# Layer norms on GpSimd a group ahead, earlier first FFN weights and a regrouped filler list in a fused attention and SwiGLU forward and backward

## The chip, the cores and the metric

One core of one Trainium2 chip. The metric is the device time of one execution in microseconds (us). Each kernel was timed in several executions on the same chip as the kernel before. A clock lies beside every execution: the mean clock that was granted to TensorE, as a share of full speed (0.96 to 0.97 in all runs of this study). The runs were made in batches, each on another chip; kernels of different batches are compared through their ratios to the kernel before.

Names used below: PE is TensorE, DVE is VectorE, ACT is ScalarE, POOL is GpSimd, SP is SyncE, which only issues DMAs here, in order. An eviction is the instruction, mostly on DVE, that copies a finished matmul result (`gen`) into another tile.

## The reference, cut to what matters

The kernel returns the output of a block and the gradients of its six inputs that it uses. Sizes: S = 2048 rows, D = 448, 16 heads of 28, F = 1792; bf16.

```python
def _fwd_reference(A_x, A_wqkv, A_wo, B_x, B_w_gate, B_w_up, B_w_down):
    xn = layernorm(A_x)                       # no scale, no bias
    q, k, v = split(xn @ A_wqkv)              # 16 heads of 28
    o = softmax(q @ k.T * 28 ** -0.5) @ v
    ffn = (silu(xn @ B_w_gate) * (xn @ B_w_up)) @ B_w_down
    return A_x + o @ A_wo + ffn               # B_x is not used

out, vjp = jax.vjp(_fwd_reference, ...)
return out, *vjp(grad_out)                    # gradients of A_x, A_wqkv, A_wo, B_w_gate, B_w_up, B_w_down
```

## The kernel before: what the change and the argument touch

The kernel has a forward part of 256 *slots* and a backward part. A slot is one tile of 128 keys against 512 queries of a group of four heads: four score matmuls on PE, then the exponentials on ACT. In the time that ACT needs for a slot, PE does other work, the *fillers*: projections of later head groups, the FFN (units a, u, dh, dw), transposes. Fillers wait in one list, `items`. They give a nominal cost in ns when they yield, and each slot spends a budget of it:

```python
    def pump(self, budget, slot):
        self.debt = min(self.debt + budget, 2 * budget)
        while self.debt > 0 and self.step(slot):
            pass
    ...
    FWD_NS = 1780
    ...
    def slot(i):
        ...                                   # 4 score matmuls, 3 exponentials
        fill.pump(FWD_NS, i)
```

So list and budget fix the order of all instructions when the program is built. At run time every engine goes through its own queue in that order and waits where data or a buffer is missing.

The filler list, first part (cut):

```python
    items = []
    for t in range(NT):                       # NT = 16
        items.append(lambda t=t: T_unit(dyT, dy_t, t))       # dy transposes
    chain = [(fc, sc) for fc in range(NFC) for sc in range(4)]
    LEAD = 2

    def ug(b, j):
        if j == 1:
            gate_ops(*chain[0])
        if j < len(chain):
            gate_ops(*chain[j])
        yield from u_unit(*b)
    for i in range(len(chain) + LEAD):
        if i < len(chain):
            items.append(lambda a=chain[i]: a_unit(*a))      # gate projection, tanh
        k = i - LEAD
        if k >= 0:
            b = chain[k]
            items.append(lambda b=b, j=i - 1: ug(b, j))      # up projection
            items.append(lambda b=b: dh_unit(*b))            # dy @ w_down.T
            if b[0] > 0 and b[1] < 3:
                items.append(lambda b=b: dw_unit(b[0] - 1, b[1]))   # weight gradients
    ...
    for g in range(G - 1, 0, -1):             # projections of groups 1..3, inserted from place lo on
        lo, hi = max(int(n_it * (g - 0.85) / 4), 26), int(n_it * (g - 0.1) / 4)
```

A weight-gradient unit reads a transposed activation `f_sp` that SP's queue has brought, and evicts through a tile with a single buffer:

```python
    def dh_unit(fc, sc):
        ...
        sp_transpose(fsp[fc][:, sc]..., t3[:]...)            # f_sp <- hda, through SP
        SP.dma_start(out=F_d[sc, :, fc], in_=t3[:])          # store of hda
    def dw_unit(fc, w):
        ...                                                  # 16 matmuls on f_sp
        if w == 0:
            o = wk.tile([P, D], BF16, name="dw_o", bufs=1)
            DVE.tensor_copy(out=o[:], in_=ps[:, :D])
            SP.dma_start(out=out_6[fc * P:(fc + 1) * P, :], in_=o[:])
```

The layer norm and the opening, twelve slots in which the rows arrive in four groups of four tiles:

```python
    def ln_norm(t):
        DVE.tensor_scalar(out=xn_sp[:, t, :], in0=xn_sp[:, t, :],
                          scalar1=mv[:, t, 0:1], scalar2=rstd[:, t:t + 1],
                          op0=ALU.subtract, op1=ALU.mult)
    ...
    slot(0)
    proj(2, 0)
    norm4(1)              # four ln_norm
    T(4, 5)               # transposes
    slot(1)
    T(6, 7)
    proj(1, 1)
    stats4(2)             # four ln_stats, then rstd on GpSimd
    slot(2)
    proj(2, 1)
    slot(3)
    ...                   # groups 2 and 3 likewise; before slot 7:
    for g in range(G):
        SP.dma_start_transpose(out=woT[:, :, g * P:(g + 1) * P], in_=wo_pad[:, g, :])
    load_fw(0)            # first FFN weights
    ...
    slot(11)
    fill.stream = [(0, u) for u in items[:10]]
    proj(0, 1)
    slot(12)
    store_wqT(0)
    proj(0, 2)
    slot(13)
    proj(0, 3)
    slot(14)
    fill.stream += [(0, u) for u in items[10:]]
    slot(15)
```

The softmax here doesn't subtract the row's maximum and nothing guards it: scores larger than these inputs give would overflow.

## Time and profile before

| | kernel before |
|---|---|
| median of the first three runs | 1489.7 us (1489.18 to 1491.23) |
| the execution that was profiled | 1484.67 us, span 1482.9, clock 0.969 |
| start of slot 12 (profile) | 49.9 us |
| start of slot 29 | 100.7 us |
| first row of the backward part | 628.2 us |

Slot 12 ends the opening, and slot 29 lies where PE has become the limit. Slot starts are read from the first score matmul of the slot in the timeline; the first backward row is the first `sb` matmul. The table of stretches, cut at these three times, shows for each engine its busy time and, in brackets, its instructions; then the clock granted to PE, the share of DMA engines busy and GB/s:

```profile
core 0: us, PE busy (x) PEld busy (x) DVE busy (x) ACT busy (x) POOL busy (x), PEclk, DMA share, GB/s
0.00:49.90 49.90, 31.39 (x184) 11.93 (x185) 30.29 (x81) 25.78 (x39) 17.49 (x43) 0.83 0.53 125
49.90:100.70 50.80, 41.75 (x322) 17.31 (x322) 35.29 (x67) 37.12 (x60) 26.37 (x44) 0.93 0.91 202
100.70:628.20 527.50, 498.13 (x3580) 192.11 (x3579) 327.92 (x569) 471.76 (x732) 217.16 (x286) 0.99 0.71 170
628.20:1482.90 854.70, 781.23 (x8593) 325.05 (x8592) 751.29 (x1304) 728.66 (x1352) 85.55 (x109) 0.97 1.00 191
```

PE is busy for 498 of 527.5 us in the third stretch: that part is bound by PE. It is busy for 73 of the first 100.7 us, partly at a lower clock: the opening is not. The end of a matmul in such a trace is worked out, not observed (the Trainium skill, Perfetto Trace Analysis, Tensor Engine Instruction, says the same); so PE's busy time is used here for comparisons only.

One group of the opening in the timeline. A line starts with its start, then its duration (both us); at the end, in brackets, the idle time of the engine before it and what released it:

```profile
27.48 0.23 POOL L226 TENSOR_SCALAR rstd<-mv 128x4 f32<-128x4 f32 x1 [12.02 <-DVE mv L231]
27.79 1.04 POOL L227 TENSOR_TENSOR rstd<-rstd,m_half 128x4 f32<-128x4 f32 x1
...
29.96 1.31 DVE L234 TENSOR_SCALAR xn_t<-xn_t,mv,rstd 128x448 bf16<-128x448 bf16 x4
30.40 0.84 PE L312 MATMUL gen<-ident_bf,xn_t 128*128 128x128 bf16 x8 [1.13 <-DVE xn_t L234]
```

Four norms take DVE 1.31 us together, and PE waits 1.13 us for them. The largest hole of PE follows later:

```profile
62.54 1.48 POOL L212 MEMSET wq_g<- 128x384 bf16 x4 [15.94 <-DMA wqT_st<-wq_g]
...
70.54 0.61 POOL L364 TENSOR_SCALAR nn<-tt 128x512 f32<-128x512 f32 x1
...
73.87 0.63 ACT L355 ACTIVATE tt<-ag 128x512 f32<-128x512 f32 x1 [5.50 <-POOL nn L366]
...
75.46 0.61 PE L583 MATMUL s_w<-QQ,KK 32*128 32x512 bf16 x2 [5.93 <-ACT eT L586]
```

GpSimd sat 15.94 us before a clear of weights; the first gate operation (`nn<-tt`, L364) came behind it in its queue at 70.54; ACT's tanh waited for a tile that the gate frees; PE waited 5.93 us for ACT. The groups by form put numbers to single operations (busy us, then mean ns of one, then idle before):

```profile
L364 POOL TENSOR_SCALAR nn<-tt 128x512 f32<-128x512 f32 x56 | 34.8, 621 | 42.4 <-DVE hda L393 17.5 <-ACT eT L588 17.4 <-ACT eT L586 4.7
L234 DVE TENSOR_SCALAR xn_t<-xn_t,mv,rstd 128x448 bf16<-128x448 bf16 x16 | 5.6, 410 | 0.8 <-POOL rstd L227 0.8
```

A norm takes DVE 410 ns. There is no norm on GpSimd here; the nearest thing is the 128x512 `nn<-tt`, 621 ns. Last, the turn from forward to backward, where the fillers are used up (SPq is SP's queue of DMAs):

```profile
609.92 1.88 PE L404 MATMUL gen<-xn_t,f_sp 128*128 128x448 bf16 x9
...
617.47 0.53 SPq L690 DMA_DIRECT2D kd<-KD_d  x1
...
628.19 0.61 PE L780 MATMUL sb<-kd,qd 32*128 32x512 bf16 x2
```

The last filler runs at 609.92, the backward part's first load is issued at 617.47, and its first row starts at 628.19.

### The profile page before, as it was taken

The numbers are of one execution on the slowest core, as the hardware profiler recorded it, in microseconds if no ns is written. First come the engines' busy times: TensorE is split into PE (matmuls) and PEld (weight loads), VectorE is DVE, ScalarE is ACT, GpSimd is POOL, SyncE is SP. The second block draws the span as 40 slices with busy tenths as digits, with TensorE's granted clock in tenths as the row PEclk, the third lists the DMA queues.
The fourth block names the chain that finished last, engine by engine and source line by source line (L and its number), as shares of the span: only waits on it lengthen the run. The fifth ranks groups of instructions, "written<-read, shape, count | busy, mean of one in ns | idle before, by whom it ended". The sixth has DMA issues, their size and how long they took to land. (4 is left out here: it accounts for less than half of the span.)

```text
span 1482.9 us, 34360 instructions
## 1 busy us (share of the span) xinstructions
PE 1352.5 (91%) x12672; PEld 546.4 (37%) x12672; DVE 1144.8 (77%) x2020; ACT 1263.3 (85%) x2180; POOL 346.6 (23%) x481
## 2 busy tenths in 40 slices
PE   5799999999999999889998889999999998999984
PEld 2333333333333333333433334433343343443341
DVE  6577666666666666388988878888989998999977
ACT  4689989988998889788988878999889998989953
POOL 2555533363434353000101001001011010000113
PEclk8999999999999999898999999999999999999997
DMA  4887956786688665599999999999999999999951
GB/s 126 173 201 192 208 129 167 184 200 146 170 189 189 150 147 141 148 197 203 208 207 199 210 200 191 203 210 225 211 177 204 196 211 209 195 199 212 178 114 51
DMA packets 698591, 269.55 MB, mean 182 GB/s; under 512 B 618080, under 2 KB 674104, under 8 KB 698424
## 3 DMA queue, kind: packets, MB, share of 16 engines
q1 hardware_dynamic: 693448, 261.24, 85.6%
q0 software_dynamic: 3568, 5.83, 1.8%
q8 instruction: 99, 1.62, 0.5%
q14 instruction: 68, 0.56, 0.1%
q10 hardware_dynamic: 1408, 0.30, 0.1%
HBM read 63.99 MB, written 58.85 MB: 83 GB/s over the span
## 5 line engine op out<-in xcount | busy, mean ns | idle before, releaser
L815 DVE TENSOR_TENSOR ds_sb<-db,e_sb 128x512 bf16<-128x512 f32 x1024 | 647.6, 684 | 65.7 <-PE db L788 23.5
L807 ACT ACTIVATE e_sb<-sb 128x512 bf16<-128x512 f32 x1024 | 554.1, 611 | 57.3 <-PE db L788 42.9
L586 ACT ACTIVATE eT<-s_w 128x1024 bf16<-128x1024 f32 x256 | 263.2, 1028 | 54.6 <-PE s_ps L583 51.2
L588 ACT ACTIVATE eT<-s_ps 128x512 bf16<-128x512 f32 x512 | 280.0, 611 | 0.0
L788 PE MATMUL db<-kd,qd 32*128 32x512 bf16 x1024 | 242.6, 386 | 12.8 <-DVE ds_sb L815 11.3
L780 PE MATMUL sb<-kd,qd 32*128 32x512 bf16 x1024 | 213.9, 390 | 6.9 <-DMA kd<-KD_d 2.9
L912 POOL TENSOR_TENSOR dq_acc<-dq_acc,dq_st 128x256 f32<-128x256 f32 x64 | 46.4, 725 | 579.8 <-ACT dq_st L910 579.8
L870 PE MATMUL acc<-ds_sb,qd 128*32 128x512 bf16 x1024 | 163.0, 395 | 0.0
L866 PE MATMUL acc<-e_sb,qd 128*32 128x512 bf16 x1024 | 161.0, 395 | 0.4 <-DVE dw_o L510 0.4
L853 ACT COPY dsT<-db 128x1024 bf16<-128x1024 bf16 x128 | 130.2, 1017 | 24.7 <-PE db L852 24.0
L583 PE MATMUL s_ps<-QQ,KK 32*128 32x512 bf16 x512 | 124.7, 390 | 4.1
L365 POOL TENSOR_TENSOR nn<-nn,ag 128x512 f32<-128x512 f32 x56 | 71.1, 1269 | 233.2 <-DVE ag L363 232.2
L1079 PE MATMUL genb<-wguT,dau_c 128*128 128x448 bf16 x448 | 117.9, 357 | 5.9 <-ACT dq_st L910 3.8
L583 PE MATMUL s_w<-QQ,KK 32*128 32x512 bf16 x512 | 101.3, 391 | 21.6 <-ACT eT L586 18.8
L780 PEld LDWEIGHTS <-qd 32*128 32x128 bf16 x1024 | 48.6, 91 | 150.9 <-issue 140.1
L404 PE MATMUL gen<-xn_t,f_sp 128*128 128x448 bf16 x448 | 99.1, 354 | 1.0 <-DVE hda L393 0.6
L404 PEld LDWEIGHTS <-f_sp 128*128 128x128 bf16 x672 | 59.8, 98 | 75.3 <-issue 25.9
L897 PE MATMUL genb<-dsT,kd 128*32 128x256 bf16 x2048 | 81.5, 280 | 6.3 <-DVE y L1031 2.8
L852 PE MATMUL db<-ident_bf,ds_sb 128*128 128x128 bf16 x1024 | 80.2, 222 | 1.8 <-DVE ds_sb L815 1.8
L852 PEld LDWEIGHTS <-ds_sb 128*128 128x128 bf16 x1024 | 68.9, 100 | 27.1 <-issue 8.4
L583 PEld LDWEIGHTS <-KK 32*128 32x128 bf16 x1024 | 29.1, 91 | 126.7 <-issue 125.6
L441 DVE TENSOR_TENSOR oacc<-gen,oacc 128x512 f32<-128x512 f32 x48 | 33.2, 691 | 53.2 <-PE gen L433 53.1
(155 smaller groups left out, 1929.0 us busy)
## 6 DMA issues: line engine op xcount, KB each, us to landing
F_d<-hda SPq DMA_DIRECT2D x56, 384.0 KB, 3.1
dau_c<-F_d SPq DMA_DIRECT2D x56, 256.0 KB, 3.7
h_c<-F_d SPq DMA_DIRECT2D x24, 256.0 KB, 3.3
qd<-QD_d SPq DMA_DIRECT2D x24, 256.0 KB, 3.8
dc<-dqkvT_d SPq DMA_DIRECT2D x12, 384.0 KB, 5.0
dsT<-ds_sb SPq DMA_TRANSPOSE x256, 4.8
wT_d<-wT_f SPq DMA_DIRECT2D x14, 256.0 KB
KD_d<-qk_sp SPq DMA_DIRECT2D x7, 512.0 KB, 3.5
```

Of the source, the lines that this page charges most:

```text
L404: PE.matmul(ps[:, :D], lhsT=fsp[fc][:, t // 4, w, t % 4, :], rhs=rhs[:, t, :], start=(t == 0), stop=(t == NT - 1))
L583: PE.matmul(sp4[hh], lhsT=KK[g][r:r + HP, kt * P:(kt + 1) * P], rhs=QQ[g][r:r + HP, qsl], start=True, stop=True, tile_position=(r, 0))
L586: ACTE.activation(out=e2[0][:], in_=wide[:], func=ACT.Exp, scale=SCALE)
L588: ACTE.activation(out=e2[1][:, j], in_=sp4[2 + j], func=ACT.Exp, scale=SCALE)
L780: PE.matmul(s_ps[:], lhsT=qside[g, qc][r:r + HP, 0, qi * P:(qi + 1) * P], rhs=kside[g, kc][r:r + HP, 0, :], start=True, stop=True, tile_po ...
L788: PE.matmul(d_ps[:], lhsT=qside[g, qc][r:r + HP, 1, qi * P:(qi + 1) * P], rhs=kside[g, kc][r:r + HP, 1, :], start=True, stop=True, tile_po ...
L807: ACTE.activation(out=est[k][:, j], in_=sps.pop((k, j))[:], func=ACT.Exp, scale=SCALE)
L815: DVE.tensor_tensor(out=ds[:, qi % 2, j], in0=dps.pop((k - 1, j))[:], in1=est[k - 1][:, j], op=ALU.mult)
L852: PE.transpose(ps[:, c, :], ds[:, 1, c // 4, (c % 4) * P:(c % 4 + 1) * P], ident_bf[:])
L853: ACTE.copy(out=dsT[b][:, 3].rearrange("p j kt s -> p (j kt) s"), in_=ps[:])
L866: PE.matmul(a[r:r + HP, :], lhsT=sp4[:, 1, r:r + HP], rhs=e[:, j, :], start=first, stop=last, tile_position=(0, r), skip_group_check=True)
L870: PE.matmul(a[r:r + HP, :], lhsT=sp4[:, 0, r:r + HP], rhs=ds[:, qi % 2, j, :], start=first, stop=last, tile_position=(0, r), skip_group_ch ...
```

## The change

Its intent: shorten the opening. The norms of groups 1 to 3 leave DVE for GpSimd and are issued a group ahead; the first FFN weights are asked for before anything else of the FFN; the weights' transposes (`woT`) are spread over the groups so that V's come ahead of them; two Q projections and twelve of the 16 dy transposes become ordinary fillers behind the first FFN units, so that the FFN chain starts two slots earlier; the first gate is issued early so that GpSimd does not block it. In addition the budget of a slot is lowered, to make the fillers last through the last slot, group 1's projections start later in the list (`LO`), and weight-gradient units of the last FFN block are moved. The core of the diff, with cuts marked:

```diff
+LO = 44
-    def ln_norm(t):
-        DVE.tensor_scalar(out=xn_sp[:, t, :], in0=xn_sp[:, t, :],
+    def ln_norm(t, eng=DVE):
+        eng.tensor_scalar(out=xn_sp[:, t, :], in0=xn_sp[:, t, :],
                           scalar1=mv[:, t, 0:1], scalar2=rstd[:, t:t + 1],
                           op0=ALU.subtract, op1=ALU.mult)
  # ... K's transposed store deferred by a list `later`; load_fw(0) split into load and fw_T(0)
         if w == 2:
             o = dwo2.pop(fc)
+            sp_flush()
     items = []
-    for t in range(NT):
+    for t in range(4):
         items.append(lambda t=t: T_unit(dyT, dy_t, t))
+    for sc in range(2, 4):
+        items.append(lambda sc=sc: qkv_unit(0, 0, sc))
     def ug(b, j):
-        if j == 1:
-            gate_ops(*chain[0])
  # ... in the loop over the chain:
+        if i == 1:
+            items.append(lambda: gate_ops(*chain[0]) or iter(()))
+            if k < 3:
+                for t in range(4 * k + 4, 4 * k + 8):
+                    items.append(lambda t=t: T_unit(dyT, dy_t, t))
-            if b[0] > 0 and b[1] < 3:
-                items.append(lambda b=b: dw_unit(b[0] - 1, b[1]))
+            if b[0] == NFC - 1:
+                todo = {1: (0,), 3: (1, 2)}.get(b[1], ())
+            else:
+                todo = (b[1],) if b[0] > 0 and b[1] < 3 else ()
+            for w in todo:
+                items.append(lambda b=b, w=w: dw_unit(b[0] - 1, w))
-        lo, hi = max(int(n_it * (g - 0.85) / 4), 26), int(n_it * (g - 0.1) / 4)
+        lo, hi = max(int(n_it * (g - 0.85) / 4), LO), int(n_it * (g - 0.1) / 4)
-    FWD_NS = 1780
+    FWD_NS = 1720
     def norm4(cc):
+        ln_rstd(cc)
         for t in range(4 * cc, 4 * cc + 4):
-            ln_norm(t)
+            ln_norm(t, POOL)
+    load_fw(0)
+    norm4(1)
     proj(1, 0, True)
     proj(0, 0)
+    for c in range(3):
+        k = 4 * c
+        t = 4 * c + 4
+        slot(k)
+        if c == 0:
+            proj(2, 0)
+        if c < 2:
+            ln_stats(t + 4)
+            ln_stats(t + 5)
+        slot(k + 1)
+        T(t, t + 1)
+        if c < 2:
+            ln_stats(t + 6)
+        slot(k + 2)
+        T(t + 2, t + 3)
+        proj(1, c + 1)
+        if c < 2:
+            ln_stats(t + 7)
+            norm4(c + 2)
+        slot(k + 3)
+        proj(2, c + 1)
+        if c == 0:
+            fw_T(0)
+        for u in later:
+            u()
+        woT_load(c)
+    store_wqT(0)
     proj(0, 1)
+    fill.stream = [(0, u) for u in items]
+    for k in range(12, 16):
+        slot(k)
+        if k == 13:
+            woT_load(3)
  # ... the old sequence of slots 0 to 15 is removed
```

More of the change, by code (lines that the diff above doesn't have):

```diff
@@ L298, in qkv_unit @@
                 st = wk.tile([P, S], BF16, name="qk_sp", bufs=1)
-                sp_transpose(st[:].rearrange("p (t r) -> p t r", r=P), src[:], nat,
+                put = lambda: sp_transpose(st[:].rearrange("p (t r) -> p t r", r=P), src[:], nat,
                              (dst[:, :, 2, :].rearrange("c p s -> p c s"),
                               st[:].rearrange("p (c s) -> p c s", c=4)))
+                if g == 0 and tq == 1:
+                    later.append(put)
+                else:
+                    put()
             elif g > 0:
@@ L338, in load_fw, with fw_T @@
         POOL.dma_start(out=w[:, 2, :D], in_=B_w_down[fsl, :])
-        sp_transpose(wT[:].rearrange("p a c d -> p (a c) d"), w[:].rearrange("p a n -> p (a n)"),
-                     (wT_d[:, fc], wT[:, 0:2].rearrange("p a c d -> p a (c d)")))
-        fw[fc] = (w4[:, 0], w4[:, 1], wT[:, 2])
+        fw[fc] = (w4[:, 0], w4[:, 1], wT[:, 2], lambda: sp_transpose(
+            wT[:].rearrange("p a c d -> p (a c) d"), w[:].rearrange("p a n -> p (a n)"),
+            (wT_d[:, fc], wT[:, 0:2].rearrange("p a c d -> p a (c d)"))))
+        if fc > 0:
+            fw_T(fc)
+    def fw_T(fc):
+        fw[fc][3]()
+    later = []
     def a_unit(fc, sc):
@@ L537 @@
             items.append(lambda b=b: dh_unit(*b))
-            if b[0] > 0 and b[1] < 3:
-                items.append(lambda b=b: dw_unit(b[0] - 1, b[1]))
+            if k < 3:
[3 more added lines that the diff above has]
+                todo = {1: (0,), 3: (1, 2)}.get(b[1], ())
+            else:
+                todo = (b[1],) if b[0] > 0 and b[1] < 3 else ()
+            for w in todo:
+                items.append(lambda b=b, w=w: dw_unit(b[0] - 1, w))
     for w in range(3):
@@ L612, in stats4, with norm4 @@
             ln_stats(t)
+        norm4(cc)
+    def norm4(cc):
         ln_rstd(cc)
-    def norm4(cc):
         for t in range(4 * cc, 4 * cc + 4):
-            ln_norm(t)
+            ln_norm(t, POOL)
     ln_stats(4)
-    norm4(0)
+    for t in range(4):
+        ln_norm(t)
     for t in range(4):
@@ L627, with woT_load @@
         ln_stats(t)
-    ln_rstd(1)
+    load_fw(0)
+    norm4(1)
     proj(1, 0, True)
     proj(0, 0)
-    slot(0)
-    proj(2, 0)
-    norm4(1)
-    T(4, 5)
-    slot(1)
-    T(6, 7)
-    proj(1, 1)
-    stats4(2)
-    slot(2)
-    proj(2, 1)
-    slot(3)
-    slot(4)
-    norm4(2)
-    T(8, 9)
-    slot(5)
-    T(10, 11)
-    proj(1, 2)
-    stats4(3)
-    slot(6)
-    proj(2, 2)
-    for g in range(G):
-        SP.dma_start_transpose(out=woT[:, :, g * P:(g + 1) * P], in_=wo_pad[:, g, :])
-    load_fw(0)
-    slot(7)
-    slot(8)
-    norm4(3)
-    T(12, 13)
-    slot(9)
-    T(14, 15)
-    proj(1, 3)
-    slot(10)
-    proj(2, 3)
-    slot(11)
-    fill.stream = [(0, u) for u in items[:10]]
-    proj(0, 1)
-    slot(12)
-    store_wqT(0)
-    proj(0, 2)
-    slot(13)
-    proj(0, 3)
-    slot(14)
-    fill.stream += [(0, u) for u in items[10:]]
-    slot(15)
+    def woT_load(g):
+        SP.dma_start_transpose(out=woT[:, :, g * P:(g + 1) * P], in_=wo_pad[:, g, :])
+    for c in range(3):
[25 more added lines that the diff above has]
+    store_wqT(0)
+    proj(0, 1)
+    fill.stream = [(0, u) for u in items]
[3 more added lines that the diff above has]
+            woT_load(3)
     qside, kside = {}, {}
```

## The prediction

> **What bounds the kernel now.** One core, 1489.7 us. The table of stretches shows four regimes. From 101 to 612 us (attention forward, FFN work as fillers between slots) PE is busy 486.3 of 510.5 us at clock 1.00: PE-bound, 2.31 us a slot; ACT needs only about 1.87 us a slot (seen where the fillers had run out). The opening is not: from 16.2 to 101.2 us PE is busy 68 of 85 us, part of it at granted clocks of 0.75 and 0.90. From 612 to 628 us the fillers are used up and PE is busy 11.3 of 16.5 us at clock 0.64. The backward and tail after that (855 us) are not touched.
>
> **What the opening loses (timeline, waits).** Twelve slots take 33.7 us. Each group of four waits for statistics, rstd (GpSimd pow, 1.04 us), four norms on DVE (1.3 us), transposes, evictions, projections. The largest hole is 69.5 to 75.5 us: the waits name ACT, but GpSimd had sat 15.9 us (46.6 to 62.5) before clearing the next projection weights, waiting for the wq transpose; the first gate operation started only at 70.5, so tanh and the filler banks stood still.
>
> **What the change does.**
> - Norms of groups 1 to 3 go to GpSimd, a group ahead. No norm there is in this trace; a one-input 128x512 operation took 0.62 us, a two-input one 1.27. Estimate: 0.6 us each, 3.8 us a group with rstd, against about 10 us available. The Trainium skill (GPSIMD Engine Reference, 4.1) calls one-input operations roughly line-rate; this agrees. PE's wait for norms (3.4 us in three) goes. I expect slot 12 at 46 instead of 49.9 us: the chain transposes, evictions, projection remains.
> - Twelve of 16 dy transpose tiles and two Q projections move behind the first FFN units; the FFN chain starts in slot 13 instead of 15, its first gate is issued before the next weights, the next group's projection weights come at filler 28 instead of 10. The 15.9 us wait and the 6 us hole should vanish. At 2.3 us a slot, slot 29 starts at 85.5 instead of 101.2 us: -15.7 us. But by the instruction order 3 us less filler work is then done.
> - Filler budget 1780 to 1720 ns a slot; total PE work is the same. By the instruction order the fillers now last through slot 255, with 45 weight-gradient matmuls (8.5 us at 0.19) after it; before, the last six slots had none. That uses some 6 us of lost PE time. But the backward's first loads wait for the last filler: before, 10.6 us passed from there to the first qd's landing; about 5 us of that becomes bare PE idleness.
>
> Sum: last filler at 85.5 + 510.5 + 3.1 + 3.0 (score and output matmuls of six slots) = 602 us; backward's first row at 612.7 instead of 628.2: -15 us, less 1.5 us for collisions.
>
> **Predicted: 1476 us, 1468 to 1485 (8 in 10).** Faster by over 2%: 0.03; within 2%: 0.96; slower: 0.01.
>
> **What would show it.** Slot 29 near 85 us; no PE hole over 2 us between 50 and 80 us; clock above 0.85 from 20 to 50 us; no 16 us GpSimd wait; GpSimd norm near 0.6 us; first backward row near 613 us; backward 855 us.
>
> **What would make it wrong.** GpSimd norms slow or blocked by DVE (over 1.5 us); PE staying cold in the opening (the Trainium skill, TensorE: Matmul & The Clock Gate, Part 1: an idle window of about 3.4 us throttles it); twelve projections now bunched in slots 38 to 50 stalling; a longer bubble at the turn.

## The result, and the profile after

| | before | after | predicted |
|---|---|---|---|
| median | 1489.4 us (1487.16 to 1491.23, 4 runs) | 1504.3 us (1502.22 to 1506.15, 4 runs) | 1476 (1468 to 1485) |
| slot 12 | 49.9 | 58.0 | 46 |
| slot 29 | 100.7 | 102.5 | 85.5 |
| first backward row | 628.2 | 643.4 | 612.7 |
| from there to the end | 854.7 | 861.0 | 855 |

The ratio is 1.010, with a 95% interval of 1.0078 to 1.0123: slower, though within 2%. A ratio is here always the mean time of a kernel's runs over the mean of the runs of the kernel before in the same rounds, so it is not quite the ratio of the medians quoted. The executions that were profiled lie 21.5 us apart and not 15: that of before (1484.67) is a further execution, faster than all four of the table, and that of after is the slowest of its four (1506.15). The traces split the 21.5 us into 8.1 before slot 12, 7.1 from there to the first backward row, and 6.2 after it; how far such a split can be trusted is said under the table of the experiments.

The table of stretches of the kernel after, cut at its own slots 12 and 29 and its first backward row (columns as above):

```profile
0.00:58.00 58.00, 32.86 (x181) 12.27 (x184) 27.34 (x69) 26.85 (x40) 36.84 (x51) 0.74 0.40 104
58.00:102.50 44.50, 37.48 (x302) 15.63 (x307) 33.61 (x63) 35.95 (x57) 27.08 (x38) 0.96 0.97 213
102.50:643.40 540.90, 496.75 (x3537) 191.68 (x3589) 332.59 (x573) 470.99 (x732) 222.12 (x296) 0.99 0.71 164
643.40:1504.40 861.00, 784.67 (x8594) 326.19 (x8592) 751.51 (x1305) 728.97 (x1352) 85.56 (x109) 0.96 1.01 192
```

GpSimd's work to slot 12 has doubled, 17.5 to 36.8 us, and PE's clock there has fallen from 0.83 to 0.74. In the third stretch PE needs about the same busy time as before (496.75 against 498.13) for a stretch 13.4 us longer. A caution: in this stretch the trace lacks some 50 matmuls (3537, where there are 3589 weight loads); busy time and idle time of PE are therefore not compared to within a few us between the two, but elapsed time is.

One group of the opening in the timeline:

```profile
27.33 0.75 DVE L290 TENSOR_SCALAR KK<-gen,cols 128x512 bf16<-128x512 f32 x1 [1.96 <-PE gen L273]
28.00 0.62 DVE L231 BATCH_NORM_STATS2 stats<-xn_t 128x6 f32<-128x448 bf16 x1
...
28.92 0.23 POOL L227 TENSOR_SCALAR rstd<-mv 128x4 f32<-128x4 f32 x1 [4.78 <-DVE mv L232]
29.24 1.04 POOL L228 TENSOR_TENSOR rstd<-rstd,m_half 128x4 f32<-128x4 f32 x1
...
30.38 7.39 POOL L235 TENSOR_SCALAR xn_t<-xn_t,mv,rstd 128x448 bf16<-128x448 bf16 x4
...
34.15 0.61 PE L317 MATMUL gen<-ident_bf,xn_t 128*128 128x128 bf16 x4 [1.50 <-POOL xn_t L235]
```

Two things are to be seen. Four norms take GpSimd 7.39 us, not 2.4; the transposes wait for each of them. Up to slot 12 PE waits 11.0 us in ten places for GpSimd's norms, where before it waited 3.4 us in three for DVE's. And they do not run a group ahead: GpSimd was idle for 4.78 us, because the last statistics of the group stand in DVE's queue behind the eviction of K (`KK<-gen`, 27.33), which itself waits for the previous group's projection. So a group takes 13.6 us: 1.46 from the start of rstd to the first norm, 7.39 for the norms, 4.78 idle. The groups by form:

```profile
L376 POOL TENSOR_SCALAR nn<-tt 128x512 f32<-128x512 f32 x56 | 35.2, 628 | 61.6 <-DVE hda L405 41.1 <-ACT tt L367 15.5 <-ACT eT L610 2.9
L235 POOL TENSOR_SCALAR xn_t<-xn_t,mv,rstd 128x448 bf16<-128x448 bf16 x12 | 22.2, 1858 | 0.3
```

The operation that the estimate was taken from kept its time (628 ns); the norm takes 1858 ns, three times that, on fewer elements and bf16. The hole near 70 us is gone, as intended: the largest idle time of PE between 50 and 80 us is 1.85 us. The turn:

```profile
631.11 0.39 PE L605 MATMUL s_w<-QQ,KK 32*128 32x512 bf16 x2
...
633.91 6.22 PE L416 MATMUL gen<-xn_t,f_sp 128*128 128x448 bf16 x32
...
637.41 0.53 SPq L709 DMA_DIRECT2D kd<-KD_d  x1
...
643.43 0.39 PE L799 MATMUL sb<-kd,qd 32*128 32x512 bf16 x2
```

The fillers now last through the last slot, and the first load of the backward part (637.41) is issued while they still run. From the last filler's end (640.1) to the first backward row 3.3 us pass. The turn got shorter, but everything before it is late.

### The profile page after: what moved, and what is told of

It is laid out like the page before. It is cut to its first block, busy times and chain, and to the rows that moved or that the text cites. A ratio compares the mean times of both kernels' runs of the same rounds, so it can differ in the third digit from the quotient of the medians.

```text
span 1504.4 us, 34282 instructions
## 1 busy us (share of the span) xinstructions
PE 1351.8 (90%) x12611; PEld 545.8 (36%) x12672; DVE 1145.0 (76%) x2008; ACT 1262.8 (84%) x2180; POOL 371.6 (25%) x493
## 3 DMA queue, kind: packets, MB, share of 16 engines
q1 hardware_dynamic: 693448, 261.24, 85.5%
## 5 line engine op out<-in xcount | busy, mean ns | idle before, releaser
L605 PE MATMUL s_w<-QQ,KK 32*128 32x512 bf16 x512 | 102.2, 395 | 16.6 <-ACT eT L608 13.6
L799 PEld LDWEIGHTS <-qd 32*128 32x128 bf16 x1024 | 48.6, 91 | 150.1 <-issue 139.2
L416 PEld LDWEIGHTS <-f_sp 128*128 128x128 bf16 x672 | 59.9, 98 | 79.7 <-issue 30.8
L446 PE MATMUL gen<-eT,VS 128*32 128x512 bf16 x1024 | 69.4, 393 | 4.3 <-DVE hda L405 1.6
```

Source lines behind the costliest of these rows:

```text
L416: PE.matmul(ps[:, :D], lhsT=fsp[fc][:, t // 4, w, t % 4, :], rhs=rhs[:, t, :], start=(t == 0), stop=(t == NT - 1))
L605: PE.matmul(sp4[hh], lhsT=KK[g][r:r + HP, kt * P:(kt + 1) * P], rhs=QQ[g][r:r + HP, qsl], start=True, stop=True, tile_position=(r, 0))
L799: PE.matmul(s_ps[:], lhsT=qside[g, qc][r:r + HP, 0, qi * P:(qi + 1) * P], rhs=kside[g, kc][r:r + HP, 0, :], start=True, stop=True, tile_po ...
```

## The experiments

Seventeen kernels were run; all gave correct results. Names with a_ start from the kernel after, names with b_ from the kernel before. In the expectations, letters stand for the theories and rivals named there. One thing in them was put too strongly: some compare "39 against 23 us" of PE idle time in the forward part. The traces of after, a_dve, a_early, a_muladd, a_dve_lo26, a_1780, b_1720, b_forms and b_forms2 hold 58 to 62 matmuls fewer than the other traces (12672), and what is missing then looks like idle time. What follows from the runs is therefore read from elapsed time for the same work and from times, or from single waits.

All measured numbers in one table, for reference below. "12 to row" is the elapsed time from slot 12 to the first backward row.

| kernel | median us | ratio to before (95%) | slot 12 | slot 29 | first row | 12 to row |
|---|---|---|---|---|---|---|
| before | 1489.4 | | 49.9 | 100.7 | 628.2 | 578.3 |
| after | 1504.3 | 1.0100 (1.0078 to 1.0123) | 58.0 | 102.5 | 643.4 | 585.4 |
| a_dve | 1495.0 | 1.0043 (1.0004 to 1.0081) | 48.8 | 94.4 | 633.8 | 585.0 |
| a_early | 1494.9 | 1.0046 (1.0013 to 1.0080) | 50.1 | 95.8 | 638.2 | 588.1 |
| a_muladd | 1494.5 | 1.0064 (1.0033 to 1.0094) | 46.0 | 92.0 | 632.1 | 586.1 |
| a_1780 | 1504.2 | 1.0119 (1.0079 to 1.0159) | 57.9 | 108.0 | 644.0 | 586.1 |
| a_dve_1780 | 1490.9 | 1.0030 (1.0005 to 1.0055) | 49.2 | 100.1 | 637.2 | 588.0 |
| a_dve_lo26 | 1496.4 | 1.0072 (1.0045 to 1.0099) | 48.6 | 98.0 | 639.3 | 590.7 |
| a_muladd_1780 | 1492.2 | 1.0044 (1.0000 to 1.0088) | 44.1 | 93.1 | 632.3 | 588.2 |
| b_1720 | 1510.2 | 1.0154 (1.0128 to 1.0181) | 50.9 | 103.6 | 651.9 | 601.0 |
| b_gate | 1489.6 | 1.0022 (0.9992 to 1.0052) | 48.9 | 106.2 | 632.9 | 584.0 |
| b_norm | 1479.3 | 0.9947 (0.9921 to 0.9973) | 46.0 | 95.1 | 627.4 | 581.4 |
| b_open | 1488.4 | 1.0005 (0.9978 to 1.0032) | 44.1 | 98.7 | 632.5 | 588.4 |
| b_norm_1720 | 1501.6 | 1.0094 (1.0051 to 1.0138) | 44.2 | 96.2 | 640.5 | 596.3 |
| b_norm_1720_o2 | 1490.8 | 1.0037 (1.0006 to 1.0067) | 45.8 | 98.0 | 632.5 | 586.7 |
| b_norm_q | 1487.7 | 1.0015 (0.9965 to 1.0064) | 45.0 | 92.0 | 628.5 | 583.5 |
| b_norm_dw | 1492.9 | 1.0044 (1.0002 to 1.0085) | 44.2 | 97.9 | 635.2 | 591.0 |

The slot columns are one execution each. Slot 29 has not the same filler work behind it where budget or order differ (3 us less is ordered by then at 1720), so that column is compared with care.

How far one trace differs from the next can be read from b_forms and b_forms2 (below), which have the forward part of the kernel before unchanged: slot 12 at 50.2 and 50.6, slot 29 at 101.4 in both, the first row at 632.1 and 631.7, and 581.9 and 581.1 us from slot 12 to it. So the trace of before is a fast one, and differences of up to some 4 us in the last two columns are not shown by one trace each: the 7.1 us of the change between slot 12 and the first row are 3.5 to 4.3 us against these two, and b_norm's first row is 4.3 to 4.7 us earlier, not 0.8. Likewise slot 12 lies between 44.1 and 46.0 in the eight kernels that have the opening of a_muladd.

### First: is the opening's loss the norm's engine, its place, or the budget?

**a_dve**: the norms back on DVE, all else as in the change.

```diff
-            ln_norm(t, POOL)
+            ln_norm(t)
```

> The changed kernel with the norms of groups 1 to 3 back on DVE, all else as changed. Theory A (the GpSimd norm, 1.86 us where 0.6 was estimated, sits on the opening's chain): slot 12 starts at 46 to 49 us instead of 58.0, the time falls from 1504 to 1491-1496 us. Rival B (the new order of stats, transposes and projections is what holds the opening, whatever engine norms): slot 12 stays at 55 us or later and the time within 4 us of 1504. The part of the loss that comes after slot 29 should stay in both.

Measured: slot 12 at 48.8, 9.2 us before the change's, and 1495.0 us. The norm's engine costs about 8.5 us by the ratios (1.0100 less 1.0043, of some 1489). With it undone the kernel is still slower than before: elapsed time from slot 12 to the first row is 585.0, as in the change (585.4).

**a_early**: the slow norms stay on GpSimd, but their statistics come ahead of the transposes, and they are issued before the K projection.

```diff
-            ln_stats(t + 4)
-            ln_stats(t + 5)
+            for u in range(t + 4, t + 8):
+                ln_stats(u)
         slot(k + 1)
         T(t, t + 1)
-        if c < 2:
-            ln_stats(t + 6)
         slot(k + 2)
         T(t + 2, t + 3)
-        proj(1, c + 1)
         if c < 2:
-            ln_stats(t + 7)
             norm4(c + 2)
+        proj(1, c + 1)
```

> The changed kernel, norms still on GpSimd, but the four stats of a group before the transposes of the one before, and its rstd and norms put in right after those transposes, ahead of the K projection. Theory A1 (GpSimd stood idle 4.8 us a group because its inputs, the last stats, are queued behind the K eviction, so the norms are not a group ahead in fact): the period of a group falls from 13.6 to 9-10 us, slot 12 at 46 to 49 us, time 1491-1497 us, though each norm still takes 1.86 us. Theory A2 (1.86 us a norm is too slow in any order): slot 12 at 54 us or later, time 1500 us or more.

Measured: slot 12 at 50.1 and 1494.9 us, nearly what a_dve gave. The two groups that follow one another so took 8.8 and 11.4 us instead of 13.6. So two things were needed for the loss together: an operation of 1.86 us, and statistics that reach it late. Either one mended recovers most of it.

**a_1780**: the change with the old budget.

```diff
-    FWD_NS = 1720
+    FWD_NS = 1780
```

> The changed kernel with the filler budget back at 1780 ns. Theory C (the lower budget costs the steady forward: after it PE idles 39 us instead of 23 us between slots 29 and 255): idle there falls to 20-28 us, the fillers end some 6 slots before the last, the time falls by 5 to 12 us to 1492-1499. Rival D (the extra idle has nothing to do with the budget but with where units fall): idle stays above 33 us and the time within 4 us of 1504.

Measured: 1504.2 us, no different from the change. On the kernel after, the budget is worth nothing in the time. That is not so for other kernels below. Its trace shows two more things. Slot 12 comes at 57.9 with the same opening at a clock of 0.82, so the clock of 0.74 in the trace of after cost no time there. And slots 12 to 29 take 50.1 us, where the change took 44.5 and the kernel before 50.8: the shortening of this stretch comes with the lower budget (a_dve and a_dve_1780 show the same, 45.6 and 50.9).

### Second: why is the norm slow on GpSimd?

**b_forms**: the kernel before with 18 GpSimd operations appended at its end, where DVE and PE are idle; it measures the cost of forms by itself.

```diff
+    sm = dict(op0=ALU.subtract, op1=ALU.mult)
+    ... POOL.tensor_scalar(out=xb, in0=xb, scalar1=pa, scalar2=pb, **sm)       # x3: bf16, per-row operands
+    ... POOL.tensor_scalar(out=xb, in0=xb, scalar1=0.5, scalar2=0.5, **sm)     # x3: bf16, constants
+    ... POOL.tensor_scalar(out=xo, in0=xf, scalar1=pa, scalar2=pb, **sm)       # x3: f32, per-row
+    ... POOL.tensor_scalar(out=xo, in0=xf, scalar1=0.5, scalar2=0.5, **sm)     # x3: f32, constants
+    ... POOL.tensor_scalar(out=xb, in0=xb, scalar1=pa, scalar2=None, op0=ALU.mult)  # x3
+    ... POOL.tensor_scalar(out=xb[:, :224], ..., scalar1=pa, scalar2=pb, **sm) # x3: half the width
```

> The kernel before with 18 extra GpSimd operations of one input at its very end, six forms three times each, with DVE idle (its total time does not matter, some 20 us more). 128x448: bf16 in and out with two per-partition pointer scalars; the same with constants; f32 with pointers; f32 with constants; bf16 with one pointer and one operation; bf16 128x224 with two pointers. If contention with DVE made the norm slow in the opening, the first form takes 0.6-0.9 us here; if the form itself is slow, 1.8 us again. If pointers are the cost, constants take 0.6 us in both types; if bf16 is, f32 takes 0.6 us with pointers as well.

Measured (one run, 1517.4 us, the 18 operations being appended), groups by form; L1308 is the norm's own form, L1314 f32 with constants, L1316 the single multiply, L1318 half the width:

```profile
L1308 POOL TENSOR_SCALAR e_sb<-e_sb,rstd 128x448 bf16<-128x448 bf16 x3 | 5.6, 1865 | 0.2
...
L1314 POOL TENSOR_SCALAR e_sb<-e_sb 128x448 f32<-128x448 f32 x3 | 5.1, 1708 | 0.3
L1316 POOL TENSOR_SCALAR e_sb<-e_sb,rstd 128x448 bf16<-128x448 bf16 x3 | 4.2, 1403 | 0.2
L1318 POOL TENSOR_SCALAR e_sb<-e_sb,rstd 128x224 bf16<-128x224 bf16 x3 | 3.3, 1112 | 0.3
```

Neither the element type (1859 in f32 with per-row operands) nor the per-row operands (1710 against 1865) nor contention with DVE, which is idle there, makes it slow. From 224 to 448 columns it grows by 753 ns: 3.36 ns per column (a column is one element in each of the 128 rows). What is left is the pair of operations: the 621 ns operation of before is a multiply and an add.

**b_forms2**: the same with other pairs.

```diff
+    ... op0=ALU.mult, op1=ALU.add         # x3, per-row;   then x3 with constants
+    ... op0=ALU.mult, op1=ALU.subtract    # x3, per-row
+    ... op0=ALU.add, op1=ALU.mult         # x3, per-row
+    ... op0=ALU.add                       # x3, one operation, per-row
+    ... op0=ALU.mult                      # x3, one operation, constant
```

> The kernel before with 18 more one-input GpSimd operations at its end, DVE idle. The first set took 1.7 to 1.9 us in every type whether with pointers or constants, yet the gate's multiply-then-add of 128x512 f32 with constants takes 0.62 us. Theory E (the pair of operations decides: subtract-then-multiply is on a slow path, multiply-then-add on a fast one): multiply-add at 128x448 bf16 takes 0.5-0.7 us with pointers and constants alike. Rival F (in-place or bf16 output or pointers make it slow together): multiply-add with pointers, in place, takes 1.4 us or more. The others (multiply-subtract, add-multiply, one add, one multiply) say how wide the fast path is; no forecast for those.

Measured, groups by form; L1304 is multiply then add, L1310 add then multiply, L1308 multiply then subtract, L1312 one add:

```profile
L1308 POOL TENSOR_SCALAR e_sb<-e_sb,rstd 128x448 bf16<-128x448 bf16 x3 | 5.6, 1868 | 0.3
L1312 POOL TENSOR_SCALAR e_sb<-e_sb,rstd 128x448 bf16<-128x448 bf16 x3 | 4.2, 1413 | 0.3
...
L1310 POOL TENSOR_SCALAR e_sb<-e_sb,rstd 128x448 bf16<-128x448 bf16 x3 | 2.2, 719 | 0.3
L1304 POOL TENSOR_SCALAR e_sb<-e_sb,rstd 128x448 bf16<-128x448 bf16 x3 | 2.2, 718 | 0.3
```

The pair decides: the same tile costs 718 ns with multiply and add in either order, 1868 with a subtract, and even one operation alone (1413) costs twice the fast pair. It is not the number of operations. The profile's page calls its durations on GpSimd rough, but the starts agree with them: in this trace three operations of L1308 and three of L1304, each with what lies between them and the next group, take 5.91 and 2.44 us.

**a_muladd**: the change with the norm written as x * rstd + (-mean * rstd).

```diff
+        s4 = slice(4 * cc, 4 * cc + 4)         # nb is a new tile
+        POOL.tensor_scalar(out=nb[:, s4], in0=mv[:, s4, 0], scalar1=-1.0, scalar2=None, op0=ALU.mult)
+        POOL.tensor_tensor(out=nb[:, s4], in0=nb[:, s4], in1=rstd[:, s4], op=ALU.mult)
         for t in range(4 * cc, 4 * cc + 4):
-            ln_norm(t, POOL)
+            POOL.tensor_scalar(out=xn_sp[:, t, :], in0=xn_sp[:, t, :],
+                               scalar1=rstd[:, t:t + 1], scalar2=nb[:, t:t + 1],
+                               op0=ALU.mult, op1=ALU.add)
```

> The changed kernel, norms still on GpSimd and in the changed order, but written x*rstd + (-mean*rstd): multiply-then-add with two pointers (two extra 128x4 operations a group, some 0.6 us). Theory E: the norm takes 0.5-0.7 us, the group's period falls from 13.6 to 9.5-10.5 us, slot 12 at 47-50 us, time 1491-1497 us as with the norms on DVE. Rival F: the norm still takes 1.4 us or more and slot 12 is at 55 us or later.

Measured, the norm's operations in the view of the tile (min, median and max ns, then the first and last start):

```profile
L644 POOL TENSOR_SCALAR xn_t<-xn_t,rstd,nb x12: 714/715/720, 17.2 to 38.3; 128x448 bf16<-128x448 bf16 x12
```

715 ns in the kernel itself, slot 12 at 46.0, the very number that was predicted for the change (to the tenth by luck: kernels with this opening show 44.1 to 46.0). The opening's loss is explained. But the whole is still 1494.5 us, slower than before by 0.33 to 0.94%, with an opening that is 3.9 us faster to slot 12 and 8.7 us faster to slot 29 (some 3 us of filler work are put off by then): something in the forward part loses more.

### Third: the budget, the later projections, the early gate

**b_1720**: only the budget of the change, on the kernel before.

```diff
-    FWD_NS = 1780
+    FWD_NS = 1720
```

> The kernel before with only the filler budget lowered to 1720 ns. With the norms back on DVE the changed kernel still is 6-8 us slower than before, and PE idles 39 us between slots 29 and 255 instead of 23-27. Theory G (any shift of where filler units fall against the slots costs the before's tuned placement 5-15 us): idle rises above 30 us here too, and the time rises by 3 us or more although the fillers now run into the empty last slots. Rival H (the lower budget is good, the new filler order is what is bad): time falls by 3 to 8 us.

Measured: 1510.2 us, ratio 1.0154. One number, which removes no work and adds none, costs 23 us, more than the whole change does. The first backward row comes at 651.9. PE's waits between 100 and 645 us by what they waited for (us in total, times, longest), in the kernel before:

```profile
PE gen L349 <- DVE dw_o L417: 2.9, 4, 1.1
PE gen L404 <- DMA f_sp<-hda: 2.5, 2, 2.2
...
PE gen L404 <- DVE dw_o L410: 0.4, 1, 0.4
```

and in b_1720:

```profile
PE gen L404 <- DMA f_sp<-hda: 9.8, 4, 3.7
...
PE gen L349 <- DVE dw_o L410: 5.8, 4, 3.6
PE gen L272 <- DVE dw_o L410: 4.1, 1, 4.1
```

At the new budget weight-gradient matmuls run into the transposes they read (9.8 us against 2.5), and PE waits 9.9 us instead of 0.4 for evictions into `dw_o` at L410. These two waits grew by 16.8 us (7.3 and 9.5), where the elapsed time from slot 12 to the first row grew by 22.7 (578.3 to 601.0; 19 to 20 against the traces of b_forms and b_forms2). As this trace lacks some matmuls, the sizes are rough, but the elapsed time is not. Where fillers meet their data is a matter of order, and the budget changes the order of everything.

**a_dve_lo26**: a_dve with the old place of group 1's projections.

```diff
-LO = 44
+LO = 26
```

> The changed kernel with norms on DVE and the next group's projections from filler 26 on as before (44 in the change). If bunching the twelve projections of group 1 between fillers 44 and 51 is what costs the rest, the time falls from 1495 to 1487-1490 us. If the rest comes from other places, or the early reload of the weights again blocks GpSimd by the wq transpose, it stays at 1492 us or more.

Measured: 1496.4 us against 1495.0 of a_dve; no gain. The bunched projections that the prediction feared are not the cause.

**b_gate**: the kernel before with only the first gate issued early.

```diff
-        if j == 1:
-            gate_ops(*chain[0])
+    def a_gate(fc, sc):
+        yield from a_unit(fc, sc)
+        gate_ops(*chain[0])
-            items.append(lambda a=chain[i]: a_unit(*a))
+            items.append(lambda a=chain[i], f=a_gate if i == 1 else a_unit: f(*a))
```

> The kernel before with only the first gate moved ahead of the second FFN weight load. If the hole of 6 us at 69.5-75.5 comes from GpSimd doing the weight load and reload ahead of the gate: it shrinks to under 2 us and the time falls by 3 to 6 us. If the 15.9 us GpSimd wait on the wq transpose alone makes it, the gate still cannot run before 66 us, and the time stays within 2 us of 1487.

Measured: 1489.6 us, nothing gained; slot 29 came at 106.2, 5.5 us later. The old hole shrank to 3.95 us and a new one came. The timeline:

```profile
82.16 4.21 SPq L202 DMA_DIRECT2D wqT_d<-wqT_st  x6
...
88.95 0.43 SPq L397 DMA_DIRECT2D F_d<-hda  x1
...
92.41 0.69 DVE L379 SCALAR_TENSOR_TENSOR hda<-ag,gen 128x512 bf16<-128x512 f32 x1 [6.83 <-DMA F_d<-hda]
...
93.75 1.90 PE L433 MATMUL gen<-eT,VS 128*32 128x512 bf16 x16 [6.50 <-DVE nn L380]
```

With the gate early, the FFN units reach SP's queue while six stores of weights occupy it (82.16 to 86.4). The store of `hda` starts late, DVE waits 6.83 us for its buffer and PE 6.50 us behind DVE. So the hole moved: what was removed at one place came up at the next, behind the queue.

**a_dve_1780**: a_dve with the old budget.

> The changed kernel with norms on DVE and the budget of 1780: what remains of the change is its order of slots and fillers. On the kernel before the budget of 1720 alone cost 23 us; with the norms on GpSimd 1780 changed nothing in the changed kernel. If the filler order is what keeps a_dve 7 us above before, this stays at 1492-1498 us. If the budget is, it falls to 1485 us or less.

Measured: 1490.9, ratio 1.0030 against 1.0043 of a_dve; within their intervals the same.

### Fourth: the opening alone, and with each other part added

**b_norm**: slots 0 to 11 of the change (with the multiply-add norm, the early first weights, the deferred store and the spread `woT` loads), but the filler list, budget, LO and gate of the kernel before.

```diff
-    slot(11)
+    # slots 0 to 11 as in the change, norm as in a_muladd
     fill.stream = [(0, u) for u in items[:10]]
     proj(0, 1)
     slot(12)
     store_wqT(0)
     proj(0, 2)
     slot(13)
+    woT_load(3)
     proj(0, 3)
     slot(14)
     fill.stream += [(0, u) for u in items[10:]]
     slot(15)
```

> As b_open but with the gate where the kernel before has it: the opening's part alone. Slot 12 at 46 us, the hole near slot 18 stays (4-8 us), time 1482-1486 us, 2 to 5 us under before. If the opening's gain is only waited away at slot 18, it is within 2 us of before.

Measured: 1479.3 us (1475.0 to 1481.5), ratio 0.9947 (0.9921 to 0.9973): faster than both kernels, the only one that is faster than the kernel before. Slot 12 comes at 46.0, and PE's clock to slot 12 is 0.89 (0.83 before, 0.74 after). Against a_muladd, which has the same opening, the filler list and budget of the change cost 1.0064 less 0.9947, some 17 us.

**b_open**: b_norm with the early gate of b_gate (5 rounds).

> A version meant to beat both: the changed kernel's opening (slots 0 to 11, early first FFN weights, norms on GpSimd as multiply-then-add a group ahead) on the filler list of the kernel before (all dy transposes first, Q projections direct, group 1 from filler 26, budget 1780); from slot 15 on TensorE's instruction order is that of before, checked. In addition the first gate is put straight after the second FFN unit. Theory G (the changed filler order and budget lose 12-16 us of idle in the steady forward, the opening itself gains): slot 12 at 46 us, no 6 us hole near 70-80 us, slot 29 at 90-93 us instead of 100.7, idle from slot 29 to 255 at 23-32 us as in before, time 1476-1481 us. Rival I (any faster opening is given back later, by other waits, whatever the order): time within 3 us of 1487.

Measured: 1488.4 us, ratio 1.0005: the early gate costs about 9 us, all that b_norm gained. The trace shows the hole of b_gate again: at 86.63 PE has waited 6.67 us behind DVE, and DVE 6.99 us for the store of `hda`; slots 12 to 29 take 54.6 us against 49.1 in b_norm. So the part of the change that was made to take away the hole is a loss on the old filler list. In the change itself no such hole is seen (the 1.85 us above), so these 9 us can't be carried over to it.

**a_muladd_1780**: a_muladd with the old budget.

> The changed kernel with the fast GpSimd norm and the budget of 1780: the change's filler order on the same opening as b_norm (1479 us). If the order alone costs what is left, 1488-1493 us. If the budget does, 1478-1483 us.

Measured: 1492.2, ratio 1.0044 against 1.0064. So budget alone is not what separates a_muladd from b_norm; with the order of the change the old budget loses nearly as much.

**b_norm_1720**: b_norm with the new budget.

```diff
-    FWD_NS = 1780
+    FWD_NS = 1720
```

> b_norm with the change's budget of 1720 alone. On the kernel before the same edit cost 23 us; if that is the budget's effect on this filler list, 1497-1504 us here. If it was tied to the old opening, 1483 us or less.

Measured: 1501.6, ratio 1.0094: 22 us lost, as b_1720 lost 23 on the old opening. The timeline of the worst place:

```profile
191.09 1.66 SPq L526 DMA_DIRECT2D out_dram<-dw_o  x4
...
194.03 0.62 DVE L423 CAST dw_o<-gen 128x448 bf16<-128x448 f32 x1 [3.87 <-DMA out_dram<-dw_o]
194.71 1.02 PE L274 MATMUL gen<-xnT,wq_g 128*128 128x512 bf16 x4 [3.83 <-DVE dw_o L423]
```

Two users of the single `dw_o` buffer come close together: DVE waits 3.87 us for the store of the first, PE 3.83 us behind DVE. In all DVE waited 6.9 us in two such places.

**b_norm_q**: b_norm with the dy transposes and Q projections among the fillers and the stream from slot 12, as in the change.

```diff
-    for t in range(NT):
+    for t in range(4):
         items.append(lambda t=t: T_unit(dyT, dy_t, t))
+    for sc in range(2, 4):
+        items.append(lambda sc=sc: qkv_unit(0, 0, sc))
+            if k < 3:
+                for t in range(4 * k + 4, 4 * k + 8):
+                    items.append(lambda t=t: T_unit(dyT, dy_t, t))
```

> b_norm with the dy transposes and two Q projections behind the first FFN units and the filler stream from slot 12. If this is the costly piece, 1486 us or more with new idle stretches after slot 16; if it is good, as the change's intent has it, 1473-1478 us.

Measured: 1487.7, ratio 1.0015, 8 us slower than b_norm by medians, 10 by ratios. Slot 29 comes 3.1 us earlier than in b_norm (92.0), as the change intended; the first row comes 1.1 us later than in b_norm (628.5). The 4.2 us between were lost on the way, about as much as traces of the same code differ; the largest single piece in the timeline is a hole of 5.73 us at 597.1 to 602.8, where weight-gradient matmuls waited for a transpose that was issued behind other DMAs in SP's queue. By times this piece is the least certain: the intervals of the two kernels overlap slightly (0.9965 to 1.0064 and 0.9921 to 0.9973), and the execution that was profiled, the fastest of its four, took 1481.8 us, as long as b_norm's.

**b_norm_dw**: b_norm with LO at 44, the last block's weight gradients moved, and the flush of SP's list.

```diff
-LO = 26
+LO = 44
+            sp_flush()
-            if b[0] > 0 and b[1] < 3:
-                items.append(lambda b=b: dw_unit(b[0] - 1, b[1]))
+            if b[0] == NFC - 1:
+                todo = {1: (0,), 3: (1, 2)}.get(b[1], ())
+            ...
```

> b_norm with group 1's projections from filler 44, the last FFN block's weight gradients moved, and the store flush ahead of each weight gradient's transpose. If this is the costly piece, 1486 us or more; if not, within 4 us of 1479.

Measured: 1492.9, ratio 1.0044: 14 us slower than b_norm. First row at 635.2, 7.8 us later than b_norm's; one hole of 4.0 us is again a wait for a transpose of `hda` behind others in SP's queue.

**b_norm_1720_o2**: b_norm_1720 with two buffers for `dw_o`, to test the mechanism seen there.

```diff
-            o = wk.tile([P, D], BF16, name="dw_o", bufs=1)
+            o = wk.tile([P, D], BF16, name="dw_o", bufs=2)
  # likewise in the second place that uses it
```

> b_norm with the budget of 1720 and two buffers instead of one for the weight-gradient eviction. If the collision on the single buffer is a real part of the budget's cost: the two waits of DVE on that store (6.9 us together) are gone, the first backward row comes 5 to 8 us earlier than b_norm_1720's 640.5, and the time falls from 1501.6 to 1493-1498 us, the rest of the cost staying. If it is masked by other waits, the time stays within 3 us of 1501.

Measured: 1490.8, ratio 1.0037 against 1.0094: the waits for the store are gone, the first row comes 8.0 us earlier, and some 8 us of the 22 are recovered. The buffer is shown to be part of the budget's cost and not all of it: 13 us against b_norm remain. Order after order runs into different waits.

## Why the prediction was wrong

The number was 1476 and the time 1504.3. The step of it that is nearest to the answer is the sum for the first backward row: predicted 612.7, measured 643.4, 30.7 us late. It splits into four terms.

1. **Slot 29 to the last filler: predicted 516.5 us, measured 537.6 (102.5 to 640.1), 21.1 us off. This is the step that failed most.** The prediction says "last filler at 85.5 + 510.5 + 3.1 + 3.0": it took the 510.5 us of the PE-bound part over from before, with "total PE work is the same", and so held that part's idle time to be independent of order and budget. The runs showed that it is not. (Some 3 us of the 21.1 lie within the spread of traces: the stretch took 511.1 us in the trace of before, 514.2 in b_forms and b_forms2.)

   On the kernel before, the budget alone costs 23 us (b_1720); on b_norm the budget costs 22, the moved weight gradients with LO 14, the dy and Q fillers 8 to 10 (the least certain) and the early gate 9 (in the traces mostly before slot 29). These costs don't add up (all of them together, a_muladd against b_norm, cost some 17): each order meets other waits. One kind of wait was shown by mending it, the single `dw_o` buffer (b_norm_1720_o2, 8 us). Two were seen in traces and not tested by themselves: transposes late in SP's ordered queue (b_norm_q, b_norm_dw, b_1720), and stores of `hda` behind weight stores (b_gate, b_open, before slot 29). The prediction allowed "1.5 us for collisions".

   In the kernel after itself the waits are many and small (no single listed wait of PE between 100 and 645 us is above 3.4 us), and the waits named so far do not make up its loss: DVE waited 1.4 us for stores of `dw_o` (7.3 in b_1720), PE 1.7 us for `f_sp` (2.5 before). What did grow, from slot 29 to the first row, are PE's waits behind DVE's operations on the FFN tiles `ag`, `nn` and `hda`: 15.2 us in all (15.4 in a_muladd), where before, b_forms, b_forms2 and b_norm show 7.2 to 7.4. With one part of the new order alone they are 7.3 to 8.8 (b_open, b_norm_q, b_norm_dw, b_norm_1720). So some 8 us of the loss lie there, by the listed waits; why the combination brings them, and what the rest is, stays open, as no run tested it.

2. **The GpSimd norm: slot 12 predicted at 46, measured at 58.0, 12.0 us off.** The prediction says "Estimate: 0.6 us each", from a 128x512 operation on one input. The count of inputs was the wrong thing to match: the operation was a multiply and add, the norm a subtract and multiply, and the pair of operations decides (718 against 1865 ns on the same tile). With the multiply-add form slot 12 came at 46.0 (a_muladd). The words "a group ahead" were wrong as well: the statistics came too late for that, and either mending alone recovers most (a_early, a_dve). The effect on the whole is 5 to 9 us of the 15 (against the change, by the ratios: a_muladd 5.4, a_early 8.0, a_dve 8.5). The item "GpSimd norms slow or blocked by DVE (over 1.5 us)" in its list of what could go wrong named the right thing; blocked they were not.

3. **Slots 12 to 29: predicted 39.5 us, measured 44.5, 5.0 us off.** "At 2.3 us a slot" is the rate of the undisturbed part. Right in it: the 15.9 us wait of GpSimd for the weights and the 6 us hole vanished, and the stretch got shorter than before's 50.8 us. (GpSimd still sits 15.5 us, now for the first tanh.) Part of the shortening is 3 us less filler work, as the prediction says, and at the old budget almost nothing of it is left (50.1 in a_1780): taking the hole away gained little time in this stretch by itself. What takes the 5 us was not tried by itself.

4. **The turn: predicted 10.6 us from the last filler to the first row, measured 3.3, 7.3 us better.** The clause "the backward's first loads wait for the last filler" was wrong: the first load was issued at 637.41 and the filler ended at 640.1.

The sum of the four is 21.1 + 12.0 + 5.0 - 7.3 = 30.8, which is the 30.7 up to rounding.

**The backward part**, predicted at 855 us, took 861.0 in the profiled execution. Its code is the same in all the kernels without appended operations, and their profiles show 851.4 to 861.0 (b_norm_q 851.4, b_norm 852.2, a_dve 860.7, after 861.0). Nothing here tells whether a part of those 6 us belongs to the change or all of it to the execution; it is left open.

Right were: the class (within 2%), the removed wait and hole, the fillers that last through the last slot, and, as things that could go wrong, slow norms and a PE that stays cold (which, by a_1780, cost no time to slot 12). The Trainium skill (TensorE: Matmul & The Clock Gate, Part 1) says that an idle window of about 3.4 us brings the clock down; most clocks to slot 12 agree in direction (0.74 with slot 12 at 58.0, 0.83 at 49.9, 0.89 at 46.0), but a_1780 shows 0.82 at 57.9, and no run here isolates a single window.

Where the expected gain went: the new opening in its good form is worth 8 us in the whole (b_norm, ratio 0.9947). The slow norm takes back 5 to 9 us of it, and the reordered fillers with the new budget some 17.

## What to carry to other kernels

When an operation moves to another engine, take its cost from a record of the same operation pair on that engine, or measure the pair by itself at the end of the kernel: here one tile cost 0.72 or 1.87 us depending on the pair alone. In a program whose order is fixed when it is built, a change of a filler budget or list is a change of the whole order behind it; don't carry over the efficiency of the old order, and test each part of a bundle by itself, because the part that was good (8 us) can be hidden by the others. Removing one wait by issuing its chain earlier only helps if the queue and the buffers behind it have room.

## What the Trainium skill lacked or had wrong

- GPSIMD Engine Reference, 4.1 Engine selection: it says that one-input elementwise operations are "roughly line-rate" on GpSimd. Here the same one-input 128x448 tile took 718 ns with multiply and add, 1868 ns with multiply and subtract, 1865 ns with subtract and multiply, 1413 ns with a single add, while DVE took 410 ns for the norm. The page doesn't say that the operation pair matters; the prediction took its 0.6 us from an operation of 0.62 us in the trace, saw the page agree, and was wrong by a factor of three.
- GPSIMD Engine Reference, 3.1 Elementwise: it gives 1.03 cycles per element where a body has at most two operations, with a clock of 1.2 GHz in its example, which makes 0.86 ns (an estimate from that page). The norm's form, two operations, measured 3.36 ns per column between 224 and 448 columns. The page doesn't say which instructions have such a body, and its list of slow cases (section 7) names no pair of operations.
- No page tells what per-row operands cost on GpSimd against constants: 1865 against 1710 ns for subtract and multiply, 718 against 569 ns for multiply and add.
